# One DMA transpose in place of TensorE for the query weights, and a new order of the whole program

## The chip, the cores and the metric

The kernel runs on one core of one Trainium2 chip. The metric is the device time of one launch in microseconds. The engines are PE (matmul; PEld is its weight load), DVE, ACT, POOL and SP; each takes its own instructions strictly in program order, and an instruction that waits holds back all that stand behind it on that engine. SP issues nearly all DMA transfers.

## The reference

Two branches over the same input x (2048 rows of 512), mixed by a gate. Cut to what matters:

```python
x = A_u                                                 # [1, 2048, 512]
g = sigmoid((x * gate_w).sum(-1, keepdims=True))
# a: state space convolution, 512 channels, 128 states, 2048 steps
K = einsum("dn,dnl,dn->dl", Cc, exp(dt*A * l), dt*Bc).real
a = irfft(rfft(u padded) * rfft(K padded))[:L] + u * Dskip
# b: linear attention, 32 heads of 16
q, k, v = split(x @ wqkv)
pq = einsum("bhsd,hdf->bhsf", q, w_phi)                 # the same for k
phi = concat(softmax(pq), softmax(-pq))
kv = einsum("bhsf,bhsd->bhfd", phi_k, v); z = phi_k.sum over s
b = ((phi_q @ kv) / (phi_q @ z + 1e-6)) @ wo
out = g * a + (1 - g) * b
```

## The kernel before, in words

The work goes through these stages, which overlap:

- Preparation. Sine tables (TB, TI, TJ), the state parameters (polar form, tables Ctab, Dtab, Gtab, and statE and statC, which go through the DRAM tensor pz). The input is loaded as UD and turned by PE into xT in eight groups of two row blocks (`xps`; each is copied from PSUM to xT by ACT or DVE).
- Folding. w_phi is the same 16x16 block for each head, so `fold` multiplies it into the weights once: PE transposes the weight block by block (`wtp`), ACT or DVE copies that to SBUF (wT), PE multiplies with the block-diagonal Wphi (`wps`), and the product is copied to WW (keys) or Wqp (queries).
- Keys. For each pair of row blocks: `pk` (matmul), Ek (exp on ACT), Zk (sum on DVE), `vp`, vr, and `kn`, which adds to kvp. At the same time the spectrum of u is made in two halves (XAu from psA, xst from psB) and written to the DRAM tensor XUd in eight pairs of stores.
- Queries and filters. Four blocks of `pq` (exp to Eq, sums and the normalising factor apm, which goes through the DRAM tensor apd and comes back as ax, the product Eq with ax, `ops`, output rows). Mixed with them, 16 units of 32 channels of the filter: E, cs, A and R on ACT and DVE, `kps` on PE, then KD, XA, XK, the product t with XUX (the spectrum read back), Zr, a turn through DRAM (Zd, ZT), `psy`, and DVE's scaled output into xT.
- The end: the last channels are turned on chip, outL (rows of the last query block) and out are stored.

Each step is a node of `Plan`. The nodes run in the order of the table ORDER (two characters a node), so this order is also that of each engine's instructions. SIDES says for each node with a choice on which of its two engines it runs (evictions: ACT or DVE), RINGS from which PSUM ring its tile comes, and WARM how many dummy matmuls (TB times the identity, result overwritten) PE runs before it. `deps` of a node are only checked against ORDER; the waits in the program come from the tiles themselves. DMA completions go through eight lanes, so a transfer also waits for the eighth one before it.

`x_psum` (sp below) is the node at which the early PSUM ring p0 closes and the rings of the keys (bk) open. It stands behind every eviction from a tile that could have been in p0, all eight of xT among them:

```python
sp = P.add("X", "x_psum", shift_psum, [n for n in P.nodes
     if n.psum is not None and not isinstance(n.psum.take[0], str)], take=["acc"], opens="bk")
...
a = P.add("PE", "pk", pk, [a] if u else [sp] + xt + kp, ...)
```

Of the kernel before, what the change touches and what calls it, by code (L numbers as in the profile page):

```python
# [13 lines left out]
BF16 = mybir.dt.bfloat16  # L14
# [56 lines left out]
class Plan:  # L71

    DIGITS = "0123456789abcdefghijklmnopqrstuvwxyzABCDEFGHIJKLMNOPQRSTUVWXYZ-_"
    ORDER = ("0H0I0J0B0C0D0M0L112P000K0S0U0V120P0W0N0_0Q0T100O0y0z0A040506010203170s0t0u0d0e0f0j0k0l0m0n0o0a0b0c0g0h0i0p0q0r0708090v0w0x2v"
             "2t2u2w2x2y140X0Y0Z1518191w2Q2R2S130R1u2T2U2V2H2X0-2W162Y2I2z2Z2J2A2-1F2K1c1a1x331l1d1m1y1n1G1H1e2F2B2_342G1v3130322C35361A1C"
             "1z1D1b1o1p1q0E0F0G2N2D2L2E2M37392O4A383a1N1L1O4H4J4I4K3b4W4Y4X4Z3d3c3e4O4L4M4N4P4Q4S4T4U3f514-3h4R551I3g3i521M4_563j4V593k50"
             "5a1J57533l5b5c5g5k5d54585o1P3m5l5p5h5e5f1B3P3Q5m5i3n5q5r3p3o5v5z5s5j5n5t1W1E3R5w1R5A3q5u1Q5D4B3u4C3v5F5E5G5B5x3w5K3x1K5L4D1r"
             "1s1t3r3s3t3y3z3A3B5O3D5y5C5H5P1S5I5J3E5M5Q3S5S5U5T5V5W5Z3I5N5R615-5X1T1U3C3J5Y62635_653K673T6c661X683L60646k6m3U6l6n3V693X6o"
             "6d6a3F3G3H3M3N3O1f1g1h3W6b3Y6p6q3Z3_6e4E3-406g1V1Y1-206h256i41421Z1_214344456r4647496f6v26274a484e4g286s4f4h222b6w292a6t6x2c"
             "2d4b4c4d4i4j4k4l4n4m2m2e4o2n6j6u6y4s2g2f232h2o2i2q4t4u2p4v2j2r2k4p4q4r4w4x4y1i1j1k242l6z2s4z8x8y6D6EaZa-a_6A6B6C8r8s8t9f9g9h"  # L80
             "8j6G8n8k8l8o8p8i8m8q4F8u4G8z8v8w8A8B6F6H8D8E6I6K8R8C6J6L8S6M6N8F8J8K8G8H6O8T8X8I8Y7b7d7c7f7haf7e7gag7i6P6Q8L8M6R6S6T6U6V6W6X"
             "6Z6-6_8-7K8_8N7j7M8P8O7L7k8Q7N8U8V90948W957lah7m7n8Zaoap7O7Qa57o7Pa9aa9192aq936Y707p7q7r7s7t7u9c9d9e7w7x7y9697a6ab71a873ad98"
             "9a99a79balaiajam74auav7vak72acae7R75anaC777S7AaD9o7T9p7BarasaE7U7V7z7W9qaIat78aw9wax7X7CaL9xaM9yaJ9r9z7D9s769A7Y7Z7-7_808183"
             "84859i9j9k9B9C9D9l9m9n9t9u9vc6c77EbY9E7GaFaGaR9F82aNc8aHaS867Hc0c17Fb-9Mc39N8789ayaAazaB888aaKb_c4798bbZ8d8caOccaP9GcdaQ9OaT"
             "c2c58ecf8fcgaU8g7I7J7ac9ca8haVcCaX9HcDchcbaYaWce9Pb99I9Qbab0b1b2eAeBeCb3b4b5eDeEeF9J9K9L9R9S9T9U9V9WdZbhd_d-biclcEcmctcue0ci"
             "cIcjcJbbbjckcvcncocwczcAcxbcbkbdblbpbxe1eVbqcpbye2cqeWe3cy9-eMe4eN9_cre5e6cscBdPbra0cQcRcSb6b7b89X9Y9Zbmbnbobebfbga1a2dQcFcG"
             "dTdUa3cHeObzeSeXe7e8e9dVcKa4cLbsbtcMcOcNcPbAd0d8bBeaebecePedeQeTeeefegcTcUcVcWcXcYbCbDbEbubvbwd1d9ehd2daeReidRejdWeUdgdodhd3"
             "dbdpd4dcdSdXdYcZc-c_bFbGbHbIbJbKd5d6d7dddedfeYdieZe_f0e-dqbLdjflbMfmbNf1drdkdseGeHeIdldmdnf2fGbOf3bPekfHf4f5dCf6eldtdudveJeK"
             "eLdwdxdydzdAdBfofrfnfpfsfqfIfMbQftfufvf7bRfwf8fJfKfNfLdDdFfadGfbdHdEf9fcfOfxfyfzfAdIfPfQfRfSfTemfUfdfgfVenfWfefhfXfYfffifBfZ"
             "f-fCf_g0dJdKdLbSbTbUbVbWbXdMdNdOeqeresetfjeoepg1fDg2euevewexeyezfkfEfFg3g4g8g9gag5g6g7")  # L90
    SIDES = ("01110100001011110000010011100010001001000000110110000000100010011000001111011100000010000000000000000100000000000000"
             "0000000100000000000000000000000000000000000100000000000")
    RINGS = ("00001011111101011010000000000000000000101010000000000000100011001010000000101101000111111010011111000110011011101111"
             "01001011")
    WARM = ("00000000430000000000000000001000060000500006000000200010001041001000044400003220010040000110000000310000000000000000"
# [98 lines left out]
def prepare(P, nc, g, evict, psum):  # L194
# [312 lines left out]
    kp = fold(P, nc, g, evict, psum, 512, lambda: g.WW[:, 0:4, :], "wT1")  # L507
    g.Wqn = fold(P, nc, g, evict, psum, 0, lambda: g.Wqp[:], "wT2")
# [3 lines left out]
def fold(P, nc, g, evict, psum, first, dst, name):  # L512

    F, fn, out = Bag(), [], []
    for h in range(2):
        box = Bag()

        def fa(h=h, box=box):
            if h == 0:
                F.wT = g.up.tile([128, 4, 512], BF16, name=name, tag="wT")  # L520
            box.ps = psum([128, 4, 512], "wtp", BF16)
            for mm in range(2):
                for kt in range(4):
                    c0 = first + 128 * (2 * h + mm)
                    nc.tensor.transpose(out=box.ps[:, mm, 128 * kt:128 * kt + 128], in_=g.wqk[:, kt, c0:c0 + 128], identity=g.ident[:])
# [1109 lines left out]
```

## Time and profile before

| | us |
|---|---|
| median of 3 runs (lowest, highest) | 250.23 (250.21, 250.74) |
| the profiled execution | 250.73 |
| its span | 248.9 |
| DVE busy | 234.3 (94%) |
| ACT busy | 221.7 (89%) |
| PE busy | 205.6 (83%) |
| POOL busy | 9.0 (4%) |
| mean granted TensorE clock | 0.962 |

Busy shares are means over stages. An instruction's time in a row reaches a little into that of the next: on DVE rows of 1.22 us follow each other at 1.14. Names such as L146 are lines of the kernel; L144 and L146 are the two engines' copy out of PSUM, L68 the activation helper, L1567 the dummy matmul.

### The profile page before, as it was taken

The page shows a single profiled execution, that of the slowest core. Times are in us where ns is not written, and L with a number is a line of the kernel's source. Part 1 is how long each engine was busy: PE and PEld are TensorE (multiplying, and loading weights), DVE is VectorE, ACT ScalarE, POOL GpSimd, SP SyncE. Part 2 cuts the span into 40 slices and gives each one's busy share as a digit, 9 for nine tenths or more (in the row PEclk, how much of TensorE's full clock was granted, in tenths as well). Part 3 has the DMA queues.
Part 4 walks back from the last instruction along what each step waited for, and adds up shares of the span by engine and source line. Part 5 has one row for each costly group of instructions (what it writes and reads, how often), then busy time and mean ns, then how long its engine had stood idle before and what let it go on. Part 6 is the DMA issues. An engine that isn't in the chain of part 4 may idle for free.

```text
span 248.9 us, 9865 instructions
## 1 busy us (share of the span) xinstructions
PE 205.6 (83%) x4383; PEld 139.2 (56%) x4409; DVE 234.3 (94%) x314; ACT 221.7 (89%) x310; POOL 9.0 (4%) x21
## 2 busy tenths in 40 slices
PE   0947999999987574799888997899998899979960
PEld 0746565655644421356656745676677567768530
DVE  7999999998999999999999998999999999998970
ACT  3999999989999999989999999999999999865650
POOL 6800000000000000000000000000000000000000
PEclk9999999999999677699999999999999999999995
DMA  6998100163521765800745039277681999872816
GB/s 189 216 204 188 32 3 4 57 179 109 158 55 46 212 208 126 237 28 24 195 131 127 13 102 286 49 212 191 197 255 48 276 215 271 176 228 40 164 28 122
DMA packets 52842, 34.86 MB, mean 140 GB/s; under 512 B 30528, under 2 KB 48320, under 8 KB 52800
## 3 DMA queue, kind: packets, MB, share of 16 engines
q1 hardware_dynamic: 52800, 34.24, 54.3%
q8 instruction: 34, 0.56, 1.0%
q14 instruction: 8, 0.07, 0.1%
HBM read 21.38 MB, written 12.58 MB: 136 GB/s over the span
## 4 chain that ended last, share of the span: by engine, by line
PE 36%; DVE 23%; ACT 20%; DMA 10%; issue 6%; SPq 2%; POOL 0%; ACTq 0%; DVEq 0%; POOLq 0%
PE kps L178 5%; PE pq L838 5%; DMA Zd<-Zr 4%; PE pk L704 4%; ACT cs L68 4%; PE vp L752 4%; ACT Ek L68 2%; DMA ZT<-Zd 2%; ACT xst L144 2%; PE psB L611 2%; DMA ax<-apd 2%; ACT L65 2%; DMA apd<-apm 2%; PE psz L1266 1%; PE psB L191 1%
## 5 line engine op out<-in xcount | busy, mean ns | idle before, releaser
L68 ACT ACTIVATE cs<-args 128x1024 bf16<-128x1024 f32 x32 | 31.0, 1064 | 0.3 <-PE args L1019 0.2
L178 PE MATMUL kps<-R,A 128*32 128x64 bf16 x1600 | 29.2, 228 | 2.1 <-DVE A L1107 0.9
L178 PEld LDWEIGHTS <-A 128*32 128x32 bf16 x1600 | 27.4, 160 | 5.3 <-issue 2.4
L1119 DVE TENSOR_TENSOR R<-E,cs 128x2048 bf16<-128x2048 bf16 x16 | 19.5, 1219 | 0.0
L1123 DVE TENSOR_TENSOR R<-E,cs 128x2048 bf16<-128x2048 bf16 x16 | 19.5, 1219 | 0.0
L1107 DVE TENSOR_TENSOR A<-Ctab,Dtab 128x2048 bf16<-128x2048 bf16 x16 | 19.5, 1219 | 0.0
L1102 DVE TENSOR_TENSOR A<-Ctab,Dtab 128x2048 bf16<-128x2048 bf16 x16 | 19.5, 1218 | 0.0
L144 ACT CAST XK<-psB 128x1024 bf16<-128x1024 f32 (+1 forms) x15 | 14.3, 987 | 4.1 <-PE psB L191 4.1
L144 ACT CAST XA<-psA 128x1024 bf16<-128x1024 f32 (+1 forms) x17 | 16.0, 973 | 2.1 <-PE psA L185 2.1
L68 ACT ACTIVATE Ek<-pk 128x512 bf16<-128x512 f32 x32 | 16.9, 600 | 1.0 <-PE pk L704 0.9
L838 PE MATMUL pq<-xT,Wqp 128*128 128x512 bf16 x64 | 17.2, 413 | 0.5 <-issue 0.5
L68 ACT ACTIVATE Eq<-pq 128x512 bf16<-128x512 f32 (+1 forms) x28 | 16.6, 673 | 0.6 <-PE pq L838 0.6
L68 ACT ACTIVATE E<-args 128x1024 bf16<-128x1024 f32 x16 | 16.6, 1038 | 0.3
L144 ACT CAST Zr<-psz 128x1024 bf16<-128x1024 f32 (+1 forms) x17 | 16.2, 990 | 0.7 <-PE psz L1302 0.3
L731 DVE TENSOR_REDUCE Zk<-Ek 128x64 f32<-128x1024 bf16 x14 | 16.4, 1210 | 0.0
L752 PE MATMUL vp<-WW,xT 128*128 128x512 bf16 x60 | 15.5, 380 | 0.4 <-issue 0.2
L704 PE MATMUL pk<-WW,xT 128*128 128x512 bf16 x57 | 15.2, 380 | 0.4 <-issue 0.2
L1237 DVE TENSOR_TENSOR t<-XUX,XK 128x2048 bf16<-128x2048 bf16 x12 | 14.5, 1221 | 0.0
L611 PE MATMUL psB<-XAu,TB 64*128 64x128 bf16 x256 | 10.6, 228 | 4.2 <-ACT xst L144 4.1
L65 ACT ACT_TABLE_LOAD x10 | 12.8, 1283 | 0.9 <-PEq L1619 0.7
L144 ACT CAST xst<-psB 128x1024 bf16<-128x1024 f32 x13 | 13.0, 1029 | 0.2 <-PE psB L611 0.2
L611 PEld LDWEIGHTS <-TB 64*128 64x128 bf16 x256 | 8.1, 100 | 8.9 <-issue 8.8
(211 smaller groups left out, 504.8 us busy)
## 6 DMA issues: line engine op xcount, KB each, us to landing
XUX<-XUd SPq DMA_DIRECT2D x28, 256.0 KB, 5.0
XUd<-xst SPq DMA_DIRECT2D x8, 512.0 KB, 3.1
ax<-apd SPq DMA_DIRECT2D x16, 256.0 KB, 4.7
Zd<-Zr SPq DMA_DIRECT2D x24, 128.0 KB, 4.0
ZT<-Zd SPq DMA_DIRECT2D x6, 512.0 KB, 5.7
UD<-in_A_u_dram SPq DMA_DIRECT2D x16, 128.0 KB, 4.2
XUd<-xst SPq DMA_DIRECT2D x8, 256.0 KB, 3.9
wqk<-in_B_wqkv_dram SPq DMA_DIRECT2D x1, 1024.0 KB, 5.5
```

The lines of the kernel that those rows point to most:

```text
L65: return self.nc.scalar.preload_act_table_set(name)
L68: return self.nc.scalar.activation(**kw)
L144: self.nc.scalar.copy(out=o, in_=i)
L178: nc.tensor.matmul(kps[32 * dj:32 * dj + 32, g4, e, :], lhsT=A[:, ka, :, :, d].rearrange("p a b -> p (a b)"), rhs=R[:, kr, d, :], start=(i ...
L611: nc.tensor.matmul(box.ps[:, c2, sl, :], lhsT=fc.TB[rows, b0:b0 + 2].rearrange("p a b -> p (a b)"), rhs=X.t[rows, k, r0 + sl].rearrange("p ...
L704: nc.tensor.matmul(box.ps[:], lhsT=xT[:, st, kt, :], rhs=g.WW[:, kt, :], start=(kt == 0), stop=(kt == 3))
L752: nc.tensor.matmul(box.ps[:], lhsT=xT[:, st, kt, :], rhs=g.WW[:, 4 + kt, :], start=(kt == 0), stop=(kt == 3))
L838: nc.tensor.matmul(box.ps[:, m - m0, :] if late else box.ps[:], lhsT=g.Wqp[:, kt, 128 * m:128 * m + 128], rhs=xT[:, 4 * b:4 * b + 4, kt, : ...
L1102: nc.vector.tensor_tensor(out=c.A[:, 0:2].rearrange("p o a b c -> p (o a) b c"), in0=g.C[U // 8][:, 0:2, :, d0 % 256:d0 % 256 + 32].rearra ...
L1107: nc.vector.tensor_tensor(out=c.A[:, 2:4].rearrange("p o a b c -> p (o a) b c"), in0=g.C[U // 8][:, 1:3, :, d0 % 256:d0 % 256 + 32].rearra ...
L1119: nc.vector.tensor_tensor(out=c.R[:, :, :, 32:64], in0=t.E[:, 1].unsqueeze(1).to_broadcast([128, 2, 32, 32]), in1=t.cs[:], op=ALU.mult)
L1123: nc.vector.tensor_tensor(out=c.R[:, :, :, 0:32], in0=t.E[:, 0].unsqueeze(1).to_broadcast([128, 2, 32, 32]), in1=t.cs[:, ::-1, :, ::-1], o ...
```

## The change

- The weight load of 512 KB for keys and 512 KB for queries becomes one of 512 KB (keys) and a DMA transpose of the queries' 512x512 block out of DRAM straight into a new tile wqT. `fold` is called with `turned` for the queries: no PE transposes and no wT copies, and its two `wps` groups read wqT.
- The two `wps` groups of the queries no longer come from the early ring p0, so they may stand after x_psum.
- A key pair's `pk` depends on its own group of xT (xt[s2]), not on all eight.
- ORDER, SIDES, RINGS and WARM are replaced as a whole.

```diff
-    ORDER = ("0H0I0J0B0C0D0M0L112P000K0S0U0V12...
+    ORDER = ("0102030K0O0L0M0P12001415130B0C0D...
...
-    P.dma("wqk", 0.5, 2.0, lambda: g.load_wqk(), rw=("", "wqk"), move=3.3)
+    P.dma("wqk", 0.5, 2.0, lambda: g.load_wk(), rw=("", "wqk"), move=1.7)
     P.dma("wv", 0.5, 2.0, lambda: g.load_wv(), rw=("", "wv"), move=1.7)
+    P.dma("wqT", 0.5, 2.0, lambda: g.load_wqT(), rw=("", "wqT"), move=2.6)
...
-    kp = fold(P, nc, g, evict, psum, 512, lambda: g.WW[:, 0:4, :], "wT1")
-    g.Wqn = fold(P, nc, g, evict, psum, 0, lambda: g.Wqp[:], "wT2")
+    kp = fold(P, nc, g, evict, psum, lambda: g.WW[:, 0:4, :], False)
+    g.Wqn = fold(P, nc, g, evict, psum, lambda: g.Wqp[:], True)
...
-    for h in range(2):
+    for h in range(0 if turned else 2):
...
-                    nc.tensor.matmul(box.ps[:, k, 128 * m:128 * m + 128], lhsT=F.wT[:, m, 128 * kt:128 * kt + 128], rhs=g.at.Wphi[:, m, :],
+                    nc.tensor.matmul(box.ps[:, k, 128 * m:128 * m + 128], lhsT=(g.wqT if turned else F.wT)[:, m, 128 * kt:128 * kt + 128], rhs=g.at.Wphi[:, m, :],
...
-        a = P.add("PE", "wps", fb, fn + [a], take=[("ps", "p0")], drop=(["wT"] if h else []), rw=("Wphi", ""))
+        a = P.add("PE", "wps", fb, fn + [a], take=["ps" if turned else ("ps", "p0")], drop=(["wT"] if h and not turned else []), rw=("Wphi wqT" if turned else "Wphi", ""))
...
-            a = P.add("PE", "pk", pk, [a] if u else [sp] + xt + kp, take=["bk"] + ([] if u else ["Ek", "Zk", "vr"]), rw=("TBn", ""))
+            a = P.add("PE", "pk", pk, [a] if u else [sp, xt[s2]] + kp, take=["bk"] + ([] if u else ["Ek", "Zk", "vr"]), rw=("TBn", ""))
...
-        g.wqk = g.up.tile([128, 4, 1024], BF16, name="wqk")
+        g.wqk = g.up.tile([128, 4, 512], BF16, name="wqk")
+        g.wqT = g.up.tile([128, 4, 512], BF16, name="wqT")
...
+        def load_wk():
+            nc.sync.dma_start(out=g.wqk[:], in_=B_wqkv[:, 512:1024].rearrange("(kt p) c -> p kt c", p=128))
+
+        def load_wqT():
+            nc.sync.dma_start_transpose(out=g.wqT[:], in_=B_wqkv[:, 0:512])
```

The sides in numbers, DVE before and after: WW 2 and 0, Wqp 0 and 1, wT 2 and 2 (now all of it), XAu 8 and 6, vb 8 and 10, xst 3 and 4, KD 1 and 0; of the small ones, oT 1 and 2, wo 2 and 1, xT from bps 0 and 2 (one 128x512, one 128x256), half a Zr 0 and 1. ACT has the rest, and its own two wT copies are gone. Dummy matmuls: 44 and 57 (before psB 8 and 27, pq 2 and 10, ops 24 and 9).

Three places. The first is SP's queue at the end of the preparation, where the transposing DMA is put in; pz, statE and statC are the state parameters, XUd<-xst the first stores of the spectrum. Before:

```order
L1501 DMA UD<-in_A_u_dram 32x16x128 x4
L345 DMA pz<-pt_195 128x512 x2
L1514 DMA WW<-in_B_wqkv_dram 128x4x512
L354 DMA statC<-pz 16x8x128 x8
L623 DMA XUd<-xst 128x4x512
L623 DMA XUd<-xst 64x4x512
```

And now:

```order
L1503 DMA UD<-in_A_u_dram 32x16x128 x4
L1519 DMA WW<-in_B_wqkv_dram 128x4x512
L346 DMA pz<-pt_297 128x512 x2
L346 DMA pz<-ppy 128x512 x2
L355 DMA statE<-pz 16x8x128 x8
L1516 DMA_TRANSPOSE wqT<-in_B_wqkv_dram 128x4x512
L624 DMA XUd<-xst 128x4x512
L624 DMA XUd<-xst 64x4x512
L624 DMA XUd<-xst 128x4x512
L624 DMA XUd<-xst 64x4x512
L355 DMA statC<-pz 16x8x128 x8
```

Both pz stores now come early, statE goes first (it stood after the last XUd store), statC follows two pairs of XUd stores, and the transpose stands between statE and the first XUd store.

The second place is SP's queue at the start of the queries; wo is the output weight, TF a copy of a table, apd and ax the normalising factor out and back. Before:

```order
L1190 DMA XUX<-XUd 128x2x512 x2
L1517 DMA wo<-in_B_wo_dram 128x4x512
L1087 DMA TF<-TJ 32x1024 x4
L1190 DMA XUX<-XUd 128x2x512 x2
L895 DMA apd<-apm 32x4x256 x2
L902 DMA ax<-apd 128x1x1024 x4
```

And now:

```order
L1191 DMA XUX<-XUd 128x2x512 x4
L896 DMA apd<-apm 32x4x256 x2
L1522 DMA wo<-in_B_wo_dram 128x4x512
L1088 DMA TF<-TJ 32x1024 x4
L903 DMA ax<-apd 128x1x1024 x4
```

wo and TF have moved from ahead of the first apd to between it and the first ax.

The third place is the end of the program. SP's last rows before (L1388 is out, L991 outL):

```order
L1388 DMA out_dram<-xT 32x12x128 x2
L1388 DMA out_dram<-xT 32x12x256 x4
L1388 DMA out_dram<-xT 32x12x128 x2
L991 DMA out_dram<-xT 32x4x384 x4
L1388 DMA out_dram<-xT 512x1x128 x4
```

and now ACT's last rows, which before ended with the scaled copies (L977) and no DMA; SP keeps two of the last four:

```order
L978 ACTIVATE xT<-bps,gT 128x384 x2
L144 CAST XK<-psB 128x512 x2
L144 CAST Zr<-psz 128x1024 x3
L144 CAST Zr<-psz 128x512
L144 CAST xT<-bps 128x2x128
L978 ACTIVATE xT<-bps,gT 128x384 x2
L992 DMA out_dram<-xT 32x4x384 x4
L1389 DMA out_dram<-xT 512x1x128 x2
```

outL and half of the last out have moved to ACT's queue, and two of the four scaled copies stand ahead of XK.

More of the change, by code (lines that the diff above doesn't have):

```diff
@@ L73 @@
     DIGITS = "0123456789abcdefghijklmnopqrstuvwxyzABCDEFGHIJKLMNOPQRSTUVWXYZ-_"
[L74 to L90, printed above, removed]
@@ L506, in prepare, with fold @@
         xt.append(evict("xT", xe, [a]))
-    kp = fold(P, nc, g, evict, psum, 512, lambda: g.WW[:, 0:4, :], "wT1")
-    g.Wqn = fold(P, nc, g, evict, psum, 0, lambda: g.Wqp[:], "wT2")
+    kp = fold(P, nc, g, evict, psum, lambda: g.WW[:, 0:4, :], False)
+    g.Wqn = fold(P, nc, g, evict, psum, lambda: g.Wqp[:], True)
     return polar, sx, xt, kp
-def fold(P, nc, g, evict, psum, first, dst, name):
-    F, fn, out = Bag(), [], []
-    for h in range(2):
+def fold(P, nc, g, evict, psum, dst, turned):
+    F, fn, out, a = Bag(), [], [], None
+    for h in range(0 if turned else 2):
         box = Bag()
@@ L519, in fa @@
             if h == 0:
-                F.wT = g.up.tile([128, 4, 512], BF16, name=name, tag="wT")
+                F.wT = g.up.tile([128, 4, 512], BF16, name="wT1", tag="wT")
             box.ps = psum([128, 4, 512], "wtp", BF16)
@@ L523, in fa @@
                 for kt in range(4):
-                    c0 = first + 128 * (2 * h + mm)
+                    c0 = 128 * (2 * h + mm)
                     nc.tensor.transpose(out=box.ps[:, mm, 128 * kt:128 * kt + 128], in_=g.wqk[:, kt, c0:c0 + 128], identity=g.ident[:])
@@ L643, in shift @@
     def shift():
-        g.UD = g.wqk = None
+        g.UD = g.wqk = g.wqT = None
         g.shift()
```

31 lines of the change are left out of this document (23 added, 8 removed).

## The prediction

> **What bounds the kernel now.** I read the head of the page and the forty slices, then the busy time by stage, then DVE's and SP's own waits, then the rows of the places that the change touches.
>
> ```profile
> span 248.9 us, 9865 instructions
> PE 205.6 (83%) x4383; PEld 139.2 (56%) x4409; DVE 234.3 (94%) x314; ACT 221.7 (89%) x310; POOL 9.0 (4%) x21
> core 0: us, PE busy (x) PEld busy (x) DVE busy (x) ACT busy (x) POOL busy (x), PEclk, DMA share, GB/s
> 0.00:25.00 25.00, 13.71 (x153) 11.97 (x154) 23.38 (x57) 20.19 (x26) 9.01 (x21) 1.00 0.99 198
> 25.00:60.00 35.00, 34.27 (x619) 20.38 (x627) 33.50 (x45) 33.81 (x65) 0.00 (x0) 1.00 0.19 53
> 60.00:100.00 40.00, 29.19 (x448) 16.68 (x449) 39.15 (x67) 39.70 (x51) 0.00 (x0) 0.87 0.49 142
> 100.00:125.00 25.00, 23.20 (x616) 14.60 (x620) 24.93 (x32) 24.03 (x42) 0.00 (x0) 0.93 0.43 115
> 125.00:150.00 25.00, 22.46 (x465) 14.52 (x459) 24.62 (x26) 24.91 (x32) 0.00 (x0) 1.00 0.37 98
> 225.00:249.00 24.00, 15.43 (x435) 10.01 (x434) 14.52 (x18) 10.67 (x19) 0.00 (x0) 0.89 0.47 90
> DVE Eq L909 <- DMA ax<-apd: 1.0, 1, 1.0
> DVE xT L1374 <- PE psy L1364: 0.9, 1, 0.9
> DVE ii L55 <- POOL idx_i L46: 1.2, 1, 1.2
> DVE ZT L1323 <- ACT Zr L144: 0.7, 1, 0.7
> ```
>
> DVE is idle for 14.6 us in all (248.9 less 234.3). Of these 1.6 lie in the first 25 us and 9.5 in the last 24; in the 200 us between hardly 3.5 us are left, and its longest waits there are the first two quoted. From 25 to 100 us ACT is as full as DVE (73.5 of 75 us against 72.65). So three things can move the end: work taken off DVE and ACT before 225 us, a new wait of DVE, and what follows DVE's last instruction. PE has room in the front (29.19 of 40 us), little from 100 to 125.
>
> **The change, part by part.** *Work on DVE and ACT.* One row stands for each kind that moves (DVE, then ACT):
>
> ```profile
> L146 DVE CAST WW<-wps 128x1024 bf16<-128x1024 f32 x2 | 2.4, 1220 | 0.0
> L146 DVE CAST XAu<-psA 128x1024 bf16<-128x1024 f32 x8 | 9.5, 1210 | 0.0
> L146 DVE CAST vb<-vp 128x512 bf16<-128x512 f32 x8 | 5.5, 686 | 0.7 <-PE vp L752 0.6
> L144 ACT CAST XAu<-psA 128x1024 bf16<-128x1024 f32 x8 | 7.9, 1018 | 0.0
> L144 ACT CAST vb<-vp 128x512 bf16<-128x512 f32 x8 | 4.8, 600 | 0.0
> L144 ACT COPY wT<-wtp 128x1024 bf16<-128x1024 bf16 x2 | 2.0, 1012 | 0.0
> ```
>
> Up to the first kps, DVE gives away two WW and two XAu casts (4 x 1.21) and takes one Wqp, one xst (the same size, 2 x 1.21) and two vb (2 x 0.69): -1.0 us. ACT takes the two WW and two XAu, gives away one Wqp, one xst and two vb, and loses the two wT copies: 2 x 1.02 - 2 x 0.60 - 2 x 1.01 = -1.2 us. Both engines are full there and both lose about as much, so the stage should end 1.0 us sooner. From there to the last psy of Q 2, DVE gives a KD cast (1.21) to ACT and takes a 128x512 xT cast (0.69): -0.5 us; an oT and a wo cast change places with ACT and cancel. In the tail DVE takes a half Zr cast and a small xT cast, about 1.0 us; ACT does one Zr half less. In the trace DVE waits there 0.7 us for exactly a Zr half of ACT and 0.3 us for psy, so I put this at nothing; uncovered it costs 1.0.
>
> *The PE side.*
>
> ```profile
> 16.10 0.61 PE L525 MATMUL wtp<-ident,wqk 128*128 128x128 bf16 x8
> 171.38 1.73 PE pq L838 x8
> 100.58 0.61 PE L1041 MATMUL args<-selE,statE 64*128 64x512 bf16 x2 [1.43 <-DVE zrow L689]
> ```
>
> Sixteen transposes go (two groups of 8 at 0.61 us). Dummy matmuls rise from 44 to 57; each is a 128x512 pass as pq's, 0.22 us: +2.9 us. Of these, psB's rise from 8 to 27 and stand in the front, where PE has 10.8 us idle in 40 from 60 us on: nothing, by that cover. pq's rise from 2 to 10 in the stage with only 1.8 us idle: 0 if they fill PE's waits (1.43 us is one of them), up to +1.8 if they don't.
>
> *The key pair's own row blocks.* I count nothing. The rule of the order that opens the new PSUM rings (sp) still depends on every xps eviction, and in the new PE order all eight xps groups still stand ahead of the first pk. What would start sooner also meets a full DVE.
>
> *The transposing DMA.* No row shows one. It stands on SP after statE's eight issues and ahead of the first XUd write.
>
> ```profile
> 22.95 3.79 SPq L354 DMA_DIRECT2D statC<-pz  x8
> 47.85 19.07 SPq L623 DMA_DIRECT2D XUd<-xst  x8
> q1 hardware_dynamic: 52800, 34.24, 54.3%
> WW<-in_B_wqkv_dram SPq DMA_DIRECT2D x1, 512.0 KB, 4.5
> ```
>
> SP has nothing to issue from 26.7 to 47.85 us, 21 us; statE's issues now end about 1 us later than statC's did (four pz writes ahead instead of two), so about 20 us of cover. Wqp's matmuls, its only reader, now stand near the end of the front, among the last psB, some 80 us in. The nearest row is the same 512 KB out of the same tensor: 4.5 us to landing, nothing on the path. The other end is a transfer cut into small pieces: 52,800 packets take 54.3% of 16 engines, 0.041 us of one engine each; 262,144 elements at that price on 16 engines are 670 us, pieces of 32 bytes (16,384) are 42 us. I take the first end, by the nearest row. The Trainium skill (VectorE: DVE Perf Modes, The three transpose paths and Rules for kernel authors) speaks against this part: it gives 1309 ns for a 128x128 block on the DMA's crossbar against 390 ns on TensorE, and says to use TensorE where a PSUM destination is fine. Sixteen blocks one after another would be 21 us by its figure (an estimate), the whole cover and a little more, and the sum below would lose about 1 us. No run here shows it.
>
> *The wk load.* 512 KB fewer are in flight while the DMA share is 0.99; SP issues the same 29 transfers up to the last block of u. ACT and DVE have other work until then: nothing. If less traffic ended the last xT copy sooner, DVE could gain part of its 1.6 us of early idle, at most 0.4 (1.2 of it is its very first wait).
>
> *The first ax.* wo's load and TF's four issues move from before the queries to between the first apd and the first ax.
>
> ```profile
> 98.51 0.47 SPq L1517 DMA_DIRECT2D wo<-in_B_wo_dram  x1
> 99.02 2.46 SPq L1087 DMA_DIRECT2D TF<-TJ  x4
> 114.45 1.24 SPq L895 DMA_DIRECT2D apd<-apm  x2
> 117.10 2.52 SPq L902 DMA_DIRECT2D ax<-apd  x4
> 113.45 0.43 DVE L881 TENSOR_TENSOR zs<-zs,den 128x256 f32<-128x256 f32 x1
> 123.73 2.36 DVE L909 TENSOR_TENSOR Eq<-Eq,ax 128x2048 bf16<-128x2048 bf16 x2
> ax<-apd SPq DMA_DIRECT2D x16, 256.0 KB, 4.7
> 102.00:106.00 4.00, 4.00 (x90) 2.16 (x92) 4.00 (x5) 4.00 (x8) 0.00 (x0) 0.81 0.97 244
> ```
>
> Now ax is issued 3.65 us after the z4 addition (L881), and its first two transfers land near 3.65 + 0.6 + 4.7 = 9.0; DVE wants them at 10.3. Then, apd's issues end at 2.25, wo and TF take 2.95, ax starts at 5.2, 1.6 later, and lands at 10.5. DVE has one R product more between the two (1.14 us), so it asks at 11.4: no wait. But 768 KB stand in the rings ahead, 3.1 us at 244 GB/s, of which 2.95 pass while SP issues. I take +0.3, between 0 and +2.2 (all 3.1 behind a spare 0.9). Behind a waiting product stand A and R of the next unit on DVE, and kps on PE.
>
> *The end.* The last stores move apart: outL (4) and half of the last out (2) go to ACT's queue, two outs stay on SP.
>
> ```profile
> 237.82 2.00 ACT L977 ACTIVATE xT<-bps,gT 128x384 bf16<-128x384 f32 x4
> 239.11 2.46 DVE L1377 TENSOR_TENSOR xT<-psy,gT 128x1024 bf16<-128x1024 f32 x3 [0.28 <-PE psy L1364]
> 239.84 3.02 SPq L991 DMA_DIRECT2D out_dram<-xT  x4
> 242.97 2.71 SPq L1388 DMA_DIRECT2D out_dram<-xT  x4
> SPq L1630 <- DMA out_dram<-xT: 2.2, 1, 2.2
> ```
>
> DVE is done at 241.57, but SP is still issuing outL until 242.86, and the four outs last until 245.68; then the last lands 2.2 us later. In the new order SP issues its two outs from 241.6 to 242.95. ACT issues outL after its last scaled copy; two of the four now stand before XK, so it ends 1.0 sooner, at 238.8. No DMA issue of ACT is in the trace; at SP's price outL takes 238.8 to 241.85 and two outs end at 243.2: 2.5 us sooner than 245.68. If the copies end no sooner, 244.3: 1.4. I take -2.2, nearer the first, since half the copies do stand earlier.
>
> The sum: -1.0 (front) - 0.5 (middle) - 2.2 (end) + 0.3 (ax) = -3.4 us. On the profiled execution, 250.73 us (1.8 outside the span), this is 247.3; that execution is 0.5 above the median of the runs, so against 250.23 it gives 246.8.
>
> **The rivals.** *The saved work turns into waits.* The front's chain passes through ACT, PE and DVE by turns (DVE 33.50 and ACT 33.81 of 35 us), and an order changed throughout may give back on one engine what another saves; only the queue at the end is shorter: 250.23 - 2.2 + 0.3 = 248.3. Against it: both engines lose work in the same stage.
>
> *The order costs what it saves.* The dummies before pq at +1.8 and ax at +2.2 instead of +0.3 make 246.8 + 3.7 = 250.5, no change. For it speaks PE at 4.00 of 4 us from 102 to 106; against it, that the first five stand where PE now waits 1.4 us.
>
> *The transposing DMA holds SP (slower).* One mechanism, on SP between statE and the first XUd write: if it takes SP or its rings for h us, XUd is late by h - 20, the two xst buffers stay full, and psB with its 16 evictions, the last part of the front, shifts by that. It decides from h = 23.4, where 3.4 us are gone. With pieces of 32 bytes, h = 42, the shift is 22 us and the time near 269; halfway, at h = 31, 258. For it: nothing shows the price. Against: the plain load of the same bytes needs 4.5. The skill's 21 us (the page above) would lie below the point.
>
> *The relaxed wait does nothing* is in my sum already.
>
> **How the numbers follow.** The likeliest case, work and end both saved, 246.8, has 0.55; its own range is 245.8 (early idle -0.4, ax at 0, end at 2.5) to 248.1 (end at 1.4, half of the tail's 1.0 uncovered). Waits instead of work, 248.3: 0.20. No change, 250.5: 0.10. Slower by the transposing DMA, or by new waits over 3.9 us: 0.12. The rest, 0.03, is a gain beyond all terms, where DVE's waits of 1.0 and 0.9 go as well (244.9). The range 244.9 to 250.7 leaves out the slower case and a little. What a measurement can tell from no change is about 0.2%, 0.5 us: faster 0.77 (the first two and the last, less a little), same 0.09, slower 0.14.
>
> **What would show it.** Right: DVE busy near 233.8 and ACT near 220; the first R about 1 us sooner than 102.17; DVE's last instruction 1.5 us sooner than 241.57; the last issue within 2 us of it, half on ACT's queue; the transposing DMA landed before 45 us, the first XUd write not later than 48. Wrong: a DVE wait for ax above 1 us, for kps or args at 100 to 125 us, XUd waiting behind the transposing DMA, issues on ACT longer than 0.75 us, or Wqp's matmuls waiting for wqT.

## The result, and the profile after

The changed kernel is slower: 253.96 us in the middle of 21 executions (249.93 to 258.14) against 250.28 (248.86 to 252.25). The ratio with its interval, 1.0081 (1.0052 to 1.0109), leaves out executions more than 1.5% above a kernel's own fastest, and here these are 12 of 21; so below each run's middle of all executions stands beside that of the kernel before on the same chip. The profiled execution after took 254.95 us. The head of its page:

```profile
span 253.1 us, 9861 instructions
PE 210.1 (83%) x4380; PEld 141.6 (56%) x4406; DVE 234.6 (93%) x316; ACT 220.8 (87%) x306; POOL 9.0 (4%) x21
```

Its stages, in the columns of the stages before:

```profile
25.00:60.00 35.00, 34.47 (x618) 20.18 (x624) 34.58 (x49) 33.85 (x65) 0.00 (x0) 1.00 0.30 77
60.00:100.00 40.00, 31.79 (x472) 17.93 (x476) 38.14 (x64) 39.35 (x50) 0.00 (x0) 0.91 0.48 139
100.00:125.00 25.00, 23.79 (x637) 15.12 (x637) 24.80 (x31) 24.85 (x43) 0.00 (x0) 1.00 0.35 99
125.00:150.00 25.00, 19.51 (x440) 13.68 (x438) 24.09 (x27) 24.19 (x31) 0.00 (x0) 1.00 0.36 107
175.00:200.00 25.00, 22.06 (x619) 16.77 (x621) 22.66 (x26) 22.30 (x28) 0.00 (x0) 1.00 0.67 195
200.00:225.00 25.00, 21.01 (x519) 16.21 (x520) 23.18 (x22) 19.36 (x21) 0.00 (x0) 0.93 0.87 228
```

DVE's work is what it was (234.6 us against 234.3); what has grown is its idle time, from 14.6 to 18.5 us. From 175 to 225 us DVE is now idle for 4.16 us of 50. The same two rows of before leave it 0.21:

```profile
175.00:200.00 25.00, 22.35 (x628) 17.30 (x628) 24.82 (x28) 24.13 (x30) 0.00 (x0) 1.00 0.69 197
200.00:225.00 25.00, 22.13 (x586) 17.61 (x588) 24.97 (x24) 20.82 (x23) 0.00 (x0) 1.00 0.83 214
```

DVE's longest waits, then ACT's:

```profile
DVE Eq L910 <- DMA ax<-apd: 3.2, 4, 1.4
DVE t L1241 <- ACT XK L144: 1.6, 1, 1.6
DVE xT L1375 <- PE psy L1365: 1.5, 2, 0.8
```

```profile
ACT xT L978 <- DVE xT L146: 3.3, 1, 3.3
```

Single instructions of DVE, set against the same ones before, tell where: the first R comes 0.58 us sooner than before, R at 193 us 0.05 later, the fourth block's product Eq 3.78 later, the last 128x512 output from psy 3.56, DVE's last instruction 5.72; behind that the kernel ends 1.5 sooner (5.8 us after it, 7.3 before). The product Eq, before and after:

```profile
196.19 1.22 DVE L909 TENSOR_TENSOR Eq<-Eq,ax 128x2048 bf16<-128x2048 bf16 x1
199.97 1.23 DVE L910 TENSOR_TENSOR Eq<-Eq,ax 128x2048 bf16<-128x2048 bf16 x1 [1.44 <-DMA ax<-apd]
```

Of its 3.78 us, 1.88 are waits (1.44 for ax, 0.44 for kps just before); the rest is order, since DVE now does two more products ahead of it.

Two places show the mechanism. DVE's tail, then ACT's:

```profile
236.38 0.42 DVE L146 CAST xT<-bps 128x256 bf16<-128x256 f32 x1
238.39 1.29 DVE L1241 TENSOR_TENSOR t<-XUX,XK 128x1024 bf16<-128x1024 bf16 x2 [1.60 <-ACT XK L144]
```

```profile
236.83 1.05 ACT L978 ACTIVATE xT<-bps,gT 128x384 bf16<-128x384 f32 x2 [3.33 <-DVE xT L146]
237.77 1.07 ACT L144 CAST XK<-psB 128x512 bf16<-128x512 f32 x2
```

The small copy xT<-bps that went to DVE stands there behind two products t; ACT's two scaled copies, now ahead of XK, need it, so ACT stands still for 3.33 us; and then DVE waits for the XK behind them. Each engine waits for the other in turn. Before, ACT goes from its last XA to XK directly and waits only for PE:

```profile
231.93 0.58 ACT L144 CAST XK<-psB 128x512 bf16<-128x512 f32 x1 [1.98 <-PE psB L191]
```

SP's queue at the fourth query block, of after, then the apd store of before:

```profile
185.52 3.77 SPq L1191 DMA_DIRECT2D XUX<-XUd  x2
189.40 1.20 SPq L896 DMA_DIRECT2D apd<-apm  x2
```

```profile
186.79 1.47 SPq L895 DMA_DIRECT2D apd<-apm  x2
```

A pair of XUX loads stands there ahead of apd and keeps SP for 3.77 us (1.1 us of it is a wait for DVE), and apd goes out 2.6 us later than before.

### The profile page after: what moved, and what is told of

Same layout as the page of the kernel before. It is cut to its first block, busy times and chain, and to the rows that moved or that the text cites. A ratio compares the mean times of both kernels' runs of the same rounds, so it can differ in the third digit from the quotient of the medians.

```text
span 253.1 us, 9861 instructions
## 1 busy us (share of the span) xinstructions
PE 210.1 (83%) x4380; PEld 141.6 (56%) x4406; DVE 234.6 (93%) x316; ACT 220.8 (87%) x306; POOL 9.0 (4%) x21
## 4 chain that ended last, share of the span: by engine, by line
PE 32%; ACT 22%; DMA 14%; DVE 13%; SPq 12%; issue 5%; ACTq 0%; DVEq 0%
DMA ax<-apd 6%; PE pk L705 6%; PE vp L753 4%; ACT Eq L68 3%; ACT cs L68 3%; PE kps L178 3%; ACT E L68 2%; ACT Zr L144 2%; ACT xst L144 2%; PE ops L929 2%; PE psA L587 2%; PE psB L612 2%; DMA XUX<-XUd 2%; DMA Zd<-Zr 2%; PE kvp L770 2%
## 5 line engine op out<-in xcount | busy, mean ns | idle before, releaser
L144 ACT CAST Zr<-psz 128x1024 bf16<-128x1024 f32 (+1 forms) x16 | 15.6, 1018 | 3.6 <-DMA Zd<-Zr 2.4
L839 PE MATMUL pq<-xT,Wqp 128*128 128x512 bf16 x64 | 16.3, 395 | 0.4 <-ACT Eq L68 0.3
L1267 PE MATMUL psz<-t,TI 128*128 128x512 bf16 x43 | 11.8, 380 | 1.4 <-ACT cs L68 0.5
L910 DVE TENSOR_TENSOR Eq<-Eq,ax 128x2048 bf16<-128x2048 bf16 x8 | 9.7, 1223 | 3.2 <-DMA ax<-apd 3.2
L144 ACT CAST xst<-psB 128x1024 bf16<-128x1024 f32 x12 | 12.2, 1025 | 0.1
```

Of the source, the lines that this page charges most:

```text
L144: self.nc.scalar.copy(out=o, in_=i)
L839: nc.tensor.matmul(box.ps[:, m - m0, :] if late else box.ps[:], lhsT=g.Wqp[:, kt, 128 * m:128 * m + 128], rhs=xT[:, 4 * b:4 * b + 4, kt, : ...
```

## The experiments

"Split" kernels run one order up to a node of the plan and the other order from there. All times in us; "diff." is the middle of the run less that of the kernel before on the same chip. A run has 6 to 12 executions, and its difference is uncertain by about 1 us either way: drawing the recorded executions again at random gives -2.4 to -0.8 for h_x, 0.4 to 1.8 for both_fix, -0.8 to 2.3 for h_q (estimates, 95%).

| run | middle (lowest, highest) | before | diff. | ratio (95%) |
|---|---|---|---|---|
| end_alone | 249.68 (248.75, 250.91) | 250.27 | -0.59 | 0.9969 (0.9943, 0.9996) |
| end_even | 249.48 (248.63, 250.62) | 250.69 | -1.21 | 0.9953 (0.992, 0.9985) |
| dead_dma | 250.32 (249.29, 250.92) | 250.53 | -0.21 | 0.9984 (0.996, 1.0007) |
| dma_alone | 256.37 (254.57, 258.77) | 250.27 | +6.10 | 1.0233 (1.0187, 1.028) |
| h_front | 255.98 (253.53, 257.80) | 250.27 | +5.71 | 1.0202 (1.0152, 1.0253) |
| h_rest | 257.97 (256.95, 259.23) | 250.27 | +7.70 | 1.031 (1.0267, 1.0353) |
| tail_fix | 252.91 (250.67, 254.28) | 250.53 | +2.38 | 1.0083 (1.0049, 1.0117) |
| sp_fix | 252.88 (251.88, 254.44) | 250.53 | +2.35 | 1.0088 (1.0051, 1.0124) |
| both_fix | 251.80 (250.52, 252.88) | 250.53 | +1.27 | 1.0041 (1.0012, 1.0069) |
| sp_mid | 251.54 (249.99, 255.55) | 250.52 | +1.02 | 1.0057 (1.0022, 1.0092) |
| warm_front | 255.17 (253.48, 260.44) | 250.52 | +4.65 | 1.017 (1.0118, 1.0223) |
| warm_ops | 252.44 (251.94, 254.73) | 250.52 | +1.92 | 1.0102 (1.0054, 1.0151) |
| h_x | 249.09 (248.26, 251.71) | 250.69 | -1.60 | 0.9943 (0.9906, 0.9981) |
| h_q | 251.58 (249.11, 254.15) | 250.52 | +1.06 | 1.0018 (0.9975, 1.0061) |
| h_q_wo | 251.17 (249.69, 252.99) | 250.66 | +0.51 | 1.0021 (0.9989, 1.0052) |
| h_late | 253.21 (251.67, 255.07) | 250.69 | +2.52 | 1.0091 (1.0052, 1.0129) |
| h_late_fix | 251.59 (250.55, 252.93) | 250.69 | +0.90 | 1.0026 (0.9995, 1.0057) |
| best | 247.83 (247.22, 249.34) | 250.66 | -2.83 | 0.9894 (0.9857, 0.993) |

**The transposing DMA.** dead_dma adds it to the kernel before, behind statC, as an extra transfer whose data nobody reads:

```diff
 def wrx(...):
+    if h == 0 and r0 == 4:
+        g.load_dead()      # dma_start_transpose of B_wqkv[:, 0:512] into the used-up half of wqk
     wr()
```

> The kernel before, untouched but for one more transfer: behind statC and ahead of the first XUd store SP issues the same transposing DMA, into the half of the weight tile that is no longer read. Nothing uses what it writes; it measures the transfer by itself. Theory (it takes about 2 us of SP's time, which is free there, and disturbs nothing): 250.3 us, within 0.3 of before, executions as close together. Rival (it holds the rings or the transfers behind it, or disturbs what runs beside it): 251.5 or more, or executions 3 us apart or more.

Measured: no difference. SP's rows and the stages of this run:

```profile
26.11 2.10 SPq L1516 DMA_TRANSPOSE wqk<-in_B_wqkv_dram  x1
47.87 12.93 SPq L623 DMA_DIRECT2D XUd<-xst  x6
```

```profile
26.00:28.00 2.00, 2.00 (x13) 1.09 (x12) 2.00 (x3) 2.00 (x5) 0.00 (x0) 1.00 0.26 61
28.00:30.00 2.00, 2.00 (x13) 1.13 (x12) 2.00 (x3) 1.92 (x5) 0.00 (x0) 1.00 1.12 238
30.00:32.00 2.00, 2.00 (x13) 1.12 (x12) 2.00 (x3) 2.00 (x4) 0.00 (x0) 1.00 0.00 1
```

It issues in 2.10 us and moves its 512 KB between 28 and 30 us at 238 GB/s; in the kernel before that stage moves nothing. So it is through some 4 us after its issue began, with 18 us of cover left. In the kernel after it issues at 27.85 us in 2.36, its bytes move from 29 to 33 us, and the first XUd store goes out at 47.76. The Trainium skill's 1309 ns for a block (VectorE: DVE Perf Modes, The three transpose paths), taken sixteen times one after another, does not hold here; its figure of 261 GB/s for a transposing DMA (DMA: Bandwidth & Descriptors, Latency and other measured facts) is near the trace's 238.

dma_alone uses the transfer in the old order: the queries' 16 transposes and two wT copies go, and I put their `wps` groups late, among the last psB.

```diff
-wtp wTe wtp wTe (queries), wps wpe wps wpe at 15 to 24 us
+wqT behind statC; wps wpe behind one xst copy, wps wpe behind one kn, at 87 and 89 us
```

> The kernel before in its own order, with the transposing DMA alone: 16 transposes of PE and two wT copies of ACT (2.0 us) go, SP issues the transpose behind statC and ahead of the first XUd write, and the queries' two wps groups and Wqp copies move behind psB near the end of the front. Theory (the transposing DMA is hidden and harmless, and work off ACT alone is worth little while DVE stays full): 249.3 to 250.3, times as close together as before's. Rival (the transposing DMA costs by what it holds or disturbs): 251 or more, with executions 3 us apart or more, as the kernel after has them.

The rival's number came, but not by its mechanism. 1.4 of the 6 us are there by DVE's first WW cast (13.14 us, 11.76 before): wc lands sooner, which I put down to the smaller weight load, and POOL's Wphi then runs beside DVE's small instructions. DVE's row before and in dma_alone, and POOL's in dma_alone:

```profile
5.45 0.29 DVE L265 TENSOR_SCALAR tgsv<-tgs,if,one 128x32 int32<-128x32 f32 x1
5.45 1.02 DVE L266 TENSOR_SCALAR tgsv<-tgs,if,one 128x32 int32<-128x32 f32 x1
```

```profile
5.29 1.15 POOL L469 TENSOR_TENSOR Wphi<-wc,mask 128x512 bf16<-128x512 bf16 x1 [0.71 <-DMA wc<-in_B_w_phi_dram]
```

3 us more come by the first R (4.48 us late), mostly from my own place for wps: DVE's Ctab waits 2.3 us behind ACT, which waits 2.2 for wps. The remaining 1.6 us are not traced. The run tells nothing of the transfer.

**The end alone.** In the kernel before:

```diff
 SIDES of outL (two halves), out (two halves)
-SP SP, SP SP
+ACT ACT, SP ACT    (end_alone)
+ACT SP,  SP ACT    (end_even)
```

> The kernel before with one edit: three entries of SIDES put both outL and one half of the last out on ACT's queue; the order stays. The prediction's term (the end gains 2.2, between 1.4 and 2.5, whatever the rest does): 248.1 us against 250.3, DVE's last product where it was (239 to 240 us), the last issue within 2 us of DVE's last instruction. Rival (in the profile after, only 1.5 us less lay between DVE's last instruction and the end, and ACT's copies end no sooner here): 248.8. Second rival (the last store's landing takes what the issues gave back): 250.3, with a landing wait of 4 us or more in place of 2.2.

> The kernel before with half of outL and half of the last out on ACT's queue, three pairs of issues so shared evenly (two and two) with SP; in the earlier run with all of outL there, ACT issued until 243.85 us, 2.9 behind DVE's last instruction, SP until 243.46. Theory (the last issue ends the kernel, and with two pairs on each queue it comes at about 242.5): 248.7, which is 1.0 less than 249.68. Rival (the last landing, 2.2 us before and 3.1 with two queues, takes what the issues give back): 249.5.

Both are faster, but by 0.59 and 1.21, not by 2.2 and 1.6; end_even came at its rival's number. ACT's issues and SP's waits in end_alone:

```profile
239.19 3.21 ACTq L991 DMA_DIRECT2D out_dram<-xT  x4
242.50 1.35 ACTq L1388 DMA_DIRECT2D out_dram<-xT  x2
```

```profile
SPq L1388 <- DVE xT L1377: 7.0, 1, 7.0
SPq L1630 <- DMA out_dram<-xT: 3.1, 1, 3.1
SPq L1388 <- DMA out_dram<-xT: 1.2, 1, 1.2
```

ACT issues as fast as SP (here 0.80 and 0.68 us each; SP before 0.76 and 0.68). But the last SP out now waits 1.2 us (1.0 in end_even) until an earlier store, issued by ACT, has landed, since the kernel's completions go through eight lanes, and the last landing takes 3.1 us (2.3 in end_even) where it took 2.2.

**The two waits of the last third.** tail_fix gives the copy back to ACT and puts the scaled copies behind XK; sp_fix moves the XUX load; both_fix does both; sp_mid has the load between apd and ax instead.

```diff
 ACT, tail (tail_fix)
+CAST xT<-bps 128x2x128
+CAST XK<-psB 128x512 x2
 ACTIVATE xT<-bps,gT 128x384 x2
-CAST XK<-psB 128x512 x2
 SP, fourth block (sp_fix)
-XUX<-XUd x2
 apd<-apm x2
 ax<-apd x4
+XUX<-XUd x2
```

> The kernel after with the tail's turn on ACT and DVE put back: the copy xT<-bps (128x256) that went to DVE is ACT's again, and ACT's first two scaled copies (L978) stand behind its two XK halves. In the profile after, ACT waits 3.33 us for that DVE copy and DVE then 1.60 us for ACT's XK. Theory (this cross-wait is 2 us of the loss): 1.5 to 2.1 us less than the kernel after, whose middle was 253.96, so about 252.0, no wait of ACT's L978 for DVE above 0.5 us, and DVE's last instruction about 4 us behind before's in place of 5.7. Rival (the time is taken up elsewhere, PE's psz or ACT's Zr setting the tail instead): 253.5 to 254.

> The kernel after with one transfer pair moved on SP: the XUX load that stands ahead of the fourth block's apd (it waits 3.5 us for its buffer at 185.5 us and holds apd and ax behind it) goes behind that block's ax. Theory (the wait for ax at 196 to 204 us comes from this): apd issued at 187.9 in place of 189.4, DVE's product Eq 1.4 us sooner, and 1 to 2 us less than the kernel after: 252 to 253. Rival (ax is late for other reasons, or the time goes to the next wait, XUX for t at 203 us or ZT at 222): 253.5 to 254.

> Both edits on the kernel after at once. Theory (the two losses add up, 2 and 1.5): 250.3 to 250.8, no slower than before by more than 0.5 us. Rival (something in the new program as a whole, such as the transposing DMA or its uneven executions, costs 2 us or more by itself): 252 or more.

> The run with both edits, but with the moved XUX pair between apd and ax in place of behind ax, where SP waits for apd's landing anyway. Theory (behind ax the pair came too late, DVE's product t waits 0.7 to 2.3 us for it): that wait goes, ax is not later, and the time falls by 0.5 to 1.0 from 251.8 to about 251.0. Rival (the wait moves on to ZT or psy): 251.8.

Against the kernel after (253.96) they give 1.05, 1.08, 2.16 and 2.42. Both edits together are clear of the noise (1.1 to 3.5, resampled as above), a single one is not quite (-0.3 to 2.7 for the tail, -0.4 to 2.8 for SP), and they add up; the tail's is smaller than expected. sp_mid is not told from both_fix: the wait for XUX falls from 0.7 to 0.3 us, as its theory had it, but the wait for ax grows from 0.3 to 1.1. With sp_fix apd goes out at 187.90, but the moved load is now late itself:

```profile
DVE t L1238 <- DMA XUX<-XUd: 2.3, 2, 1.6
```

In both_fix's profiled execution DVE's last instruction starts 1.4 us behind before's in place of 5.7; but that execution is the fastest of its twelve (250.52), and the one of after is slower than its middle, so the 4.3 us between them overstate the gain. The theory of both_fix (250.8 at most) missed and its rival holds in part: 1.27 stay.

**Which part of the order.** The first two splits, at the node x_up:

```diff
-before's order, sides, rings, dummies
+after's up to x_up, then before's       (h_front)
+before's up to x_up, then after's       (h_rest)
```

> The new order, sides, rings and dummies up to the end of the front (the node x_up, about 100 us in), then the old ones to the end, the end's queue included; with the transposing DMA. Theory (the new front is worth what the traces show there, 0.6 to 1.2 us by the first R products, and what loses stands behind it): 249.3, DVE's first R at 101.0 to 101.6 us and every later milestone about 1 us sooner than before. Rival (the front's gain is handed back to waits that the old rest also meets): 250.3. Second rival (the front is what makes the executions uneven and slow): 252 or more.

> The other half: the old order up to the end of the front (with the transposing DMA, as in the run that adds it alone), then the new order, sides, rings and dummies to the end, the end's queue included. Theory (the loss is behind the front: +3.5 us where DVE's product waits for ax and XUX at 185 to 205 us, +2 where DVE and ACT wait for each other in the tail, -1.5 at the end): 253.5 to 255, executions 3 us apart or more. Rival (the loss comes from how the new rest meets the new front): 250 to 251.

Neither tells which part loses, and no forecast for them was met by its mechanism. h_rest has the front of dma_alone, its first R 4.35 us late. h_front has a seam of my making: the last kvp stands on PE ahead of the first filter arguments. PE's wait there:

```profile
PE kvp L770 <- DVE vr L762: 7.0, 1, 7.0
```

The later splits cut where the two orders have nearly the same nodes behind them: x_keys (about 100 us) and x_q (about 150 us). h_late and h_late_fix have no transposing DMA at all.

```diff
+after's up to x_keys, then before's     (h_x)
+after's up to x_q, then before's        (h_q)
+the same, wo and TF ahead of the first apd   (h_q_wo)
+before's up to x_q, then after's        (h_late)
+the same with both edits of both_fix    (h_late_fix)
```

> The new program as it is up to the end of the third query block (the node x_q, about 150 us), then the old order, sides, rings and dummies to the end, the end's queue included. Theory (the new front gains about 1 us in a good execution and loses it again before 150 us, and all else that is lost lies behind 150 us): 250.2 to 251.0. Rival (the first 150 us cost 1.5 us or more in the middle of the executions, by their unevenness): 252 or more, with executions 3 us apart. Second rival (the first 150 us keep their gain): 249.3.

> The old program, with the queries' weights turned by TensorE, up to the end of the third query block (x_q, about 150 us), then the new order, sides, rings and dummies to the end, the end's queue included. Theory (the new last third alone loses 2 us by the tail's cross-wait and 1 by the XUX pair ahead of apd, and wins 0.6 at the end): 252.3 to 253, every milestone up to 150 us within 0.1 us of before's. Rival (the last third is only slow behind the new front): 250.5.

> The same with both edits of the earlier runs (the tail's turn put back, the XUX pair behind ax). Theory (these two are all that the new last third loses): 249.7 to 250.3. Rival (it also loses by transfers that land late for DVE, XUX and the turn Zd and ZT between 200 and 230 us, as the run with the warmed front shows with 4 us): 251 or more.

> The new front up to the node x_keys (about 100 us, the first query products among it), then the old order to the end. Theory (the new front wins 0.7 us by the first R product, the old rest keeps it, and its PE clock alone makes the executions uneven by 1 us): 249.5 to 250, the executions within 2 us. Rival (the unevenness of the first 150 us lies in the front): 251.5, executions 4 us apart or more.

> The run with the new first 150 us and the old rest (251.58, 249.1 to 254.2), with wo's load and TF's four issues put back ahead of the first apd, as in the old order; nothing else. Theory (the prediction's step on the first ax was mis-sized: with wo and TF between apd and ax, the first ax comes 1.2 us later, the second block's apd and ax behind it too, and DVE's waits for ax, 0.9 us in the profiled execution, grow with every late landing): 249.8 to 250.5, executions within 3 us. Rival (the stage loses by its work and its PE order: 0.7 us more of copies on DVE up to 168 us, kps later): 251.3 or more, spread as before.

These place the loss. The new front wins 1.60 (h_x). With the stage up to x_q added, 1.06 are lost (h_q): that stage costs 2.66. The last third alone costs 2.52 (h_late). The sum, -1.60 + 2.66 + 2.52 = 3.58, is near what the whole kernel shows (253.96 - 250.28 = 3.68). That it comes within 0.1 us is luck: resampled, the stage lies between 0.5 and 4.1 and the last third between 1.3 and 3.6, and h_q by itself is not told from the kernel before (ratio 0.9975 to 1.0061). h_q came between its theory and its rival, h_late_fix at its rival, and h_x won more than its theory had. Of the last third the two edits take back 1.62 (h_late to h_late_fix), 0.90 stay though the end wins 0.6 there; in that trace DVE waits 1.2 us for XUX, 0.8 for psy and 1.2 for Zr. In the middle stage, putting wo and TF back gains 0.4 (h_q to h_q_wo), which is nearer the rival than the theory of that run and not told from nothing (-1.7 to 1.9). One 128x512 copy moved from ACT is 0.68 us more work of a full DVE; this is its row in h_q, and h_x has none:

```profile
147.13 0.68 DVE L146 CAST xT<-bps 128x512 bf16<-128x512 f32 x1
```

About 1.5 of the 2.66 stay unexplained. In the two profiled executions (251.49 and 249.19 us, near the middles) h_q loses 1.05 us to h_x between the first R and 168 us, 0.45 up to 228 and 0.65 in the tail. The copy (0.6 to the start of the next row) and small waits make up most of these 2.15 us: DVE's listed waits behind the first R add up to 3.2 us in h_q and 2.1 in h_x, none above 0.7. What lengthens them no run shows; PE's order, the PSUM rings and the dummies before pq (2 and 10) changed in this stage too and were not taken apart.

**PE's clock.** warm_front adds 40 dummy transposes to both_fix, around the place of the queries' 16; warm_ops gives it the old numbers of dummies ahead of ops.

```diff
 def tx(T8=T8, box=box):          (warm_front)
+    idle({0: 16, 4: 8}.get(T8, 0))     # transposes of wqk into the unused half of the tile
     for t in range(8): nc.tensor.transpose(... g.UD ...)
+    idle({4: 16}.get(T8, 0))
 WARM of ops                      (warm_ops)
-9 in all
+24 in all
```

> The run with both edits (251.8) and, in addition, dummy transposes in the front where the queries' 16 transposes used to keep PE busy: 16 ahead of the first xps group, 8 ahead of the second and 16 behind it, all into the unused half of that tile. In four executions of the new program the first R product lies between 0.69 us sooner and 0.26 later than before, and PE's groups of four psri transposes take 1.06 us in the late one and 0.60 in the soonest; in three executions of the old front it lies within 0.02 us. Theory (without the transposes PE stays at its slow clock there in some executions, and the new front, unlike the old, waits for PE): the psri groups at 17 us and later take 0.60 to 0.64, the first R comes at 101.3 to 101.6, and the middle of the executions falls by 0.4 to 0.9 to about 251.1, with less spread. Rival (the unevenness comes from the loads' landings): 251.8, with the same spread.

> The run with both edits, with the old kernel's numbers of dummies ahead of ops (24 in place of 9; 3.3 us of PE more between 100 and 160 us). Theory (between 125 and 150 us PE is busy 19.5 of 25 us in place of 22.5, so its clock falls to half for 4 us now here, now there: at 128 to 132 us in one execution, at 201 to 205 in another; the dummies prevent that): no slow clock between 105 and 160 us, 0.3 to 0.8 less than 251.8. Rival (PE has no room there, and the dummies delay kps and so DVE's A and R): 252.5 or more.

In the front the profiled execution of warm_front looks as its theory said. PE's rows there (psri are four transposes each of a state parameter), and in sp_fix, the same program up to here without the dummies:

```profile
17.34 0.60 PE L366 MATMUL psri<-ident,Are 128*128 128x128 bf16 x4
...
18.72 0.60 PE L366 MATMUL psri<-ident,Cre 128*128 128x128 bf16 x4
```

```profile
20.27 1.06 PE L366 MATMUL psri<-ident,Cre 128*128 128x128 bf16 x4
```

The first R on DVE, before and in warm_front, then in sp_fix:

```profile
102.17 1.22 DVE L1119 TENSOR_TENSOR R<-E,cs 128x2048 bf16<-128x2048 bf16 x1
100.77 1.22 DVE L1125 TENSOR_TENSOR R<-E,cs 128x2048 bf16<-128x2048 bf16 x1
```

```profile
102.43 1.22 DVE L1120 TENSOR_TENSOR R<-E,cs 128x2048 bf16<-128x2048 bf16 x1
```

But this one execution does not show that the dummies do it: both_fix, without them, has 0.60 in its own, with the first R at 101.48. In ten executions of the new front without the dummies the first R lies from 0.81 us sooner than before to 0.68 later; in the two late ones (sp_fix, best) the Cre group begins at 20.3 us and takes 1.06, and DVE's pmag waits 1.0 and 1.1 us for it; in the others it takes 0.60 to 0.79, or (h_q_wo) 1.06 but from 19.6 us on, and pmag waits 0.5 at most. In six executions of the old front the first R lies within 0.05 us. The Trainium skill (TensorE: Matmul & The Clock Gate, Part 1: The HAM clock gate) has PE at half clock until a window of about 3.4 us has been busy, with a window that runs free, so that the same kernel may warm up sooner or later; the two durations and their change from one execution to the next agree.

The clock as granted (the third number from the end) agrees too. Two stretches of 1 us each of best, then of end_alone, which has the old front:

```profile
17.00:18.00 1.00, 1.00 (x10) 1.00 (x9) 1.00 (x3) 0.81 (x2) 0.00 (x0) 0.50 1.35 215
21.00:22.00 1.00, 1.00 (x7) 1.00 (x6) 0.06 (x1) 0.51 (x1) 0.00 (x0) 0.50 1.13 389
```

```profile
17.00:18.00 1.00, 1.00 (x12) 1.00 (x11) 1.00 (x3) 1.00 (x2) 0.00 (x0) 0.50 1.28 229
21.00:22.00 1.00, 0.60 (x6) 0.64 (x7) 1.00 (x3) 1.00 (x2) 0.00 (x0) 1.00 0.08 17
```

So the theory behind warm_front, that the queries' transposes had kept PE warm, is not borne out: with all sixteen of them, the old front is at 0.50 for some 3.4 us between 16 and 21 us in five of its six executions, and PE's groups take 1.0 us there. It does not matter to DVE, because the Cre group comes only at 21.4 us, when the slow stretch is over:

```profile
21.39 0.60 PE L365 MATMUL psri<-ident,Cre 128*128 128x128 bf16 x4 [0.46 <-DVE pt L378]
```

In the new front this group stands about 1 us earlier or more, and where the slow stretch lasts beyond it (to 22.9 us in best) DVE waits for it. (In sp_fix the clock's column shows 1.00 although its groups take 1.06 us; there the durations are the evidence.)

In warm_front the first R comes 1.40 us sooner than before. But the kernel as a whole became slower than both_fix, 255.17 against 251.80: what was won is lost behind 110 us. DVE's waits in warm_front:

```profile
DVE xT L1380 <- PE psy L1370: 3.4, 2, 1.9
DVE t L1243 <- DMA XUX<-XUd: 2.9, 2, 1.6
DVE xT L1383 <- PE psy L1370: 1.8, 1, 1.8
```

Why an earlier front makes these later is not settled. warm_ops has no slow clock from 105 to 240 us and is 0.64 slower than both_fix all the same, hardly clear of the noise: its theory fails, and that PE has no room there, its rival, is likely but not shown by itself.

**The version that beats both.** The new front, the old rest and the even end:

```diff
+after's up to x_keys, then before's; outL ACT SP, out SP ACT
```

> The new front (to x_keys), the old rest, and the end's issues shared evenly between ACT's queue and SP's. Theory (the two gains, 1.4 and 1.0, lie in different places and add up): 248.0, DVE's last product at about 237.6 and the last issue within 2 us of its end. Rival (the end's gain goes into the landing): 248.8.

Measured 247.83, ratio 0.9894 (0.9857 to 0.993): the gains add up (-1.60 - 1.21 = -2.81 against -2.83; so close a match is luck, as above). Its profiled execution is the slowest of the six (249.34), the one with the late first R.

## Why the prediction was wrong

The forecast was 246.8, the kernel needs 253.96. The step that failed is what the sum holds for waits behind the front: 0.3 for the first ax and nothing for the rest of the new order, the tail's exchange of casts among it. In its place the runs show 2.66 us lost from x_keys to x_q and 2.52 in the last third. Two new waits of the last third are shown by taking them out (2.16 together); what causes most of the 2.66 stays open. Step by step:

- *Work on DVE and ACT, front -1.0*: borne out; h_x gains 1.60 (0.8 to 2.4), though its trace has 0.81 of it by the first R and the rest in shorter waits behind. *Middle -0.5*: wrong in place and sign up to 150 us. DVE's 0.69 for the xT copy is paid there, and the KD copy that it gives away stands only behind (178 us before). DVE's busy time came to 234.6 us where 233.8 was forecast.
- *In the tail DVE takes a half Zr cast and a small xT cast ... I put this at nothing*: this step failed. I priced the casts (1.0 uncovered) and not what is queued on either side of them. ACT's scaled copies now need DVE's cast and stand ahead of the XK that DVE needs: 3.33 us of ACT (1.98 before, for PE), 1.60 of DVE, 1.05 us of the time.
- *The end, -2.2*: the mechanism was right and the size off; alone it is worth 0.59. The sum of issues was worked as if each transfer went out at once; the wait for a completion lane (1.2) and a longer last landing (3.1 for 2.2) were left out, though the kernel's lanes were known. In the profiled execution of the whole kernel, where two of the scaled copies stand earlier, the end is 1.5 shorter; their price is paid in the tail.
- *The first ax, +0.3*: not confirmed. The 0.4 of h_q_wo is within the noise, and in the traces of after and h_q the first Eq does not wait for ax; the wait is at the second block (0.88 us in after).
- *PE side*: the dummies at nothing is not shown. No run takes out those added before psB and pq; with the old numbers before ops the kernel is 0.64 slower, hardly clear of the noise. Sixteen transposes less were counted as harmless; they had not kept PE's clock up, but with the new order DVE can meet PE in its slow stretch, and the first R spreads over 1.5 us.
- *The transposing DMA, nothing* and its slower rival: the first is right (-0.21), the rival refuted.
- *The key pair's own row blocks* and *the wk load*: no run tells them apart from the front; in the old order the kernel with the smaller load lost 1.4 us to POOL beside DVE.
- What the sum did not contain at all: the order behind 110 us. The three places read were those that the diff's words named. SP's XUX load ahead of apd (1.08) could have been read from the new order; of the stage up to 150 us (2.66) at least the xT copy's 0.6.
- The rival *the saved work turns into waits* was the right idea with the wrong bound: I let the waits cost at most what the work saved (248.3), but a new order can lose more than it won. Nothing keeps DVE's idle time from growing past its 14.6 us.

So the miss of 7.2 us is, in sizes that are each uncertain by 1 us or more, 1.6 at the end, 2.1 in the two new waits of the last third, 2.9 in the stage up to 150 us (2.66 lost where 0.2 were to be won) and about 1.2 in other waits of the last third, less 0.6 that the front won beyond its forecast.

## What to carry to other kernels

When a whole order is replaced, cut it at the nodes where both orders have done the same and run the halves: three splits placed a loss of 3.7 us, and joining the winning part with the old rest and an even end beat the kernel before by 1.1%. Compare the sum of the terms with their noise before trusting it. When a cast moves to another engine, read what stands ahead of it there and who waits for it, not its price. Look at the spread of the executions too, and at both orders before blaming what was taken out: PE ran slow in the old front as well, but the first R repeated within 0.05 us, and the work that DVE needs of PE came after the slow stretch; in the new front it spreads over 1.5 us.

## What the runs showed of the hardware that I had not expected

- A 512 KB transposing DMA out of DRAM takes 2.1 us to issue (2.36 in after), moves at 238 GB/s and is done some 4 us after its issue began (dead_dma).
- A DVE tensor_scalar of 128x32 takes 1.02 us in place of 0.29 while POOL's Wphi runs: it ends at 6.47, POOL at 6.44 (dma_alone). The Trainium skill (SBUF — State Buffer, Who interferes with whom) says that the two share a pair of ports, which one holds for its whole instruction; the two ends agree.
- Four 128x128 transposes on PE take 1.06 or 0.60 us at the same place of the same program, from one execution to the next, with the granted clock at 0.50 or 1.00 (best, after).
- ACT issued the stores of the end at 0.44 to 1.03 us each, and SP, beside it, at 0.40 to 1.03 (end_alone, end_even, best, after).
